# Softcapped attention feeding a mixture of causal attention experts: the exponentials of a pair of heads in one instruction, and a new order of score fills

## The chip, the cores and the metric

The kernel runs on one core of a Trainium2 chip. The metric is the time of the device for one execution, in microseconds (us); lower is better. The engines are named as in the profile: PE multiplies matrices (TensorE) and writes its results to PSUM, DVE (VectorE) and ACT (ScalarE) work elementwise, POOL (GpSimd) converts inputs and masks, and SP issues most loads and stores. Each engine works through its own queue in order; semaphores hold an instruction back until what it needs is there.

## The reference

Stage A is attention with a soft cap, for 8 batches and 12 heads of 448 tokens and 64 dimensions, cap 30:

```python
scores = scale * np.matmul(q, k.transpose(0, 1, 3, 2))
scores = cap * np.tanh(scores / cap)
attn = softmax(scores)            # exp, divided by its sum
x = matmul(attn, v)               # heads put side by side: (8, 448, 768)
```

Stage B treats each batch of x with four experts of one 64-wide head each: causal attention over projections of x, each token taking its two best experts, weighted by a softmax over their two gate values. The result is the sum of the weighted experts after an output projection, (8, 448, 768).

## The kernel before

**Pairs.** Stage A takes two heads at a time, 48 pairs, six to a batch. SP loads q, k and v of two pairs at once, some pairs ahead; POOL casts them to 16 bits (`a_cast`, L378, and `a_castv`, L399; pairs 0 and 1 partly on DVE); PE transposes queries and keys (`a_tr`, L410) and DVE moves the transposes to SBUF.

**Scores.** Scores lie with keys on the partitions and 448 queries along the row. Each head has three blocks of 128 keys; the remaining 64 keys of both heads make one shared "tail" block. So a pair has seven blocks of 448 columns. They are filled by PE in four parts (`fill`, L444): for a two-block part, one matmul per head, and each uses only the 64 partition rows on which its head's dimensions lie, one the lower and one the upper half; the tail is one matmul over all rows. A part occupies one of only two score buffers (`ps_score`, L280), two PSUM banks each. ACT reads a part with tanh (`tanh`, L462), which frees the buffer, and writes 16-bit values to SBUF; ACT then takes exp over several blocks at once (`expo`, L472). `HALF` (L441) gives the blocks of each part: 2, 2, 2, and the tail 1 last. Before the change a pair has two exponentials: over the four blocks of parts 0 and 1, and over the three of parts 2 and 3.

**ACT's order.** It is written out in the list `prog` (L894): T is a tanh, E an exp, X an exp of stage B, S marks where a new pair begins. For a common pair p:

```
T(p,0) T(p,1) [X part 0] E(p-1,1) [X part 1] T(p,2) T(p,3) E(p,0)
```

The X parts are there for two pairs of each batch (`EXPB`, L891). The first pair begins with nothing to finish; the last pair issues all four tanh, then the remaining three exponentials.

**After the exp.** PE multiplies the probabilities with the values (`a_pv_mm`, L481): for each of four query windows seven matmuls, six of a head's block and one of the tail with a value tile that holds both heads. A last value column of ones gives the sum; DVE takes its reciprocal and scales (`a_pv_out`, L516). PE transposes the result into x.

**Stage B.** For a finished batch PE computes projections for queries and keys of two experts at a time (r = 0, 1), values and gates. The causal scores of two experts e are filled into two score buffers of at most 1024 columns (`b_fill`, L675), laid out by `COL`: part 0 holds the tails and the three blocks of expert 0, part 1 the three blocks of expert 1. The experts of a pair lie on the two row halves of PE. ACT takes the exp (`b_exp`, L697), POOL zeroes what lies above the diagonal with `affine_select`, and products, transposes and the output projection follow, the last with a store by SP.

**The order on PE** comes from a planner that runs while the kernel is built (`Plan`, L18). It keeps an estimate of when each engine gets how far. For each score fill (`do_fill`, L920) it notes when the buffer comes free and when ACT will need it, and `pump` (L86) first issues other work through `step` (L65): of the units that could start soonest, the one with the earliest due time, as long as it ends before `latest`. `slot` (L943) and `batch` (L980) put units of stage A and B into the list with costs, dependencies and due times; loads and casts are issued in `slot` too. After the last pair's fills, `last_batch` (L1026) takes all that is left and orders it with a search over a list scheduler (`Graph`).

Of the kernel before, what the change touches and what calls it, by code (L numbers as in the profile page):

```python
# [11 lines left out]
f16 = mybir.dt.float16  # L12
# [5 lines left out]
class Plan:  # L18
# [46 lines left out]
    def step(self, until, latest):  # L65


        at = {}
        for u in self.work:
            r = self.ready(u)  # L70
            if r is not None:
                at[u["key"]] = max(r, self.pe)
        if not at:
            return False
        first = min(at.values())
        u = min(
            (u for u in self.work if at.get(u["key"], 1.0e9) <= first + 0.3),
            key=lambda u: u["due"],
        )
        if first > until or first + u["pe"] > latest:  # L80
            return False
        self.work.remove(u)
        self.emit(u)
        return True
# [156 lines left out]
def kernel(  # L241
# [199 lines left out]
    HALF = (2, 2, 2, 1)  # L441
    score = {}

    def fill(p, i):  # L444
        qt, kt = qkt[p]
        sc = ps_score.tile([128, 2, 512], f32, name=f"s{i}_{p}", tag="score")
        if i == KC:
            del qkt[p]
            nc.tensor.matmul(sc[:, 0, 0:S], kt[:, 0:128], qt, start=True, stop=True)  # L449
        else:  # L450
            for g in range(2):
                r = slice(64 * g, 64 * (g + 1))
                nc.tensor.matmul(  # L453
                    sc[:, g, 0:S], kt[r, 128 * (i + 1) : 128 * (i + 2)], qt[r, :],
                    start=True, stop=True,
                )
        score[(p, i)] = sc
# [4 lines left out]
    def tanh(p, i):  # L462
        g = i // 2
        n = HALF[i]
        if i % 2 == 0:
            y[(p, g)] = actp.tile([128, 4 - g, S], f16, name=f"y{g}_{p}", tag=f"y{g}", bufs=2)
        nc.scalar.activation(  # L467
            y[(p, g)][:, 2 * (i % 2) : 2 * (i % 2) + n, :], score.pop((p, i))[:, 0:n, 0:S],
            AF.Tanh, scale=isc / capf,
        )  # L470

    def expo(p, g):  # L472
        pt = actp.tile([128, 4 - g, S], f16, name=f"p{g}_{p}", tag=f"p{g}")
        nc.scalar.activation(pt, y.pop((p, g)), AF.Exp, scale=capf)  # L474
        pr[(p, g)] = pt
# [5 lines left out]
    def a_pv_mm(p, i, n, parts):  # L481

        if n == 0 and 0 in parts:
            pvs[p, i] = bank([128, 2, 2, Dh + 1], f32, f"pv{i}_{p}")
        pv = pvs[p, i]
        w = WIN[2 * i + n]
        for h in parts:
            pt = pr[(p, h)]
            for c in (2 * h, 2 * h + 1):
                if c == KC:  # L490
                    nc.tensor.matmul(  # L491
                        pv[:, n, :, :], pt[:, 2, w : w + 128], vtz[p % 12],
                        start=False, stop=True, skip_group_check=True,
                    )
                    continue
                for g in range(2):
                    nc.tensor.matmul(  # L497
                        pv[:, n, g, :], pt[:, 2 * (c % 2) + g, w : w + 128],
                        v16[p % 12][:, g, c, :],
                        start=(n == 0 and c == 0 and g == 0), stop=False, skip_group_check=True,  # L500
                    )
# [14 lines left out]
    def a_pv_out(p, i):  # L516
        a_pv_rc(p, i)
        a_pv_xk(p, i)
        if i == 1:
            del pr[(p, 0)], pr[(p, 1)]  # L520
# [152 lines left out]
    COL = {(0, 0): 64, (0, 1): 512, (0, 2): 832, (1, 1): 1024, (1, 2): 1344, (1, 0): 1536}  # L673

    def b_fill(b, r, g):  # L675
# [12 lines left out]

        if g == 0:
            for e in range(2):  # L690
                block(e, 0, KM, TL, 64 * e)
        for (e, c), o in COL.items():
            if e == g:
                block(e, o - 1024 * g, 128 * c, 128, 0)
        s["sc", r, g] = sc

    def b_exp(b, r, g):  # L697
# [3 lines left out]
        n = 1024 - 64 * g  # L701
        o0 = 64 + 1024 * g
# [3 lines left out]
        blocks = [(o, 0, 128, 128) for (e, _), o in COL.items() if e == g]  # L706
# [203 lines left out]
    def dur(o):  # L910
# [4 lines left out]
        return 0.09 + 0.373 * (4 - o[2]) if o[0] == "E" else 0.055 + 0.373 * HALF[o[2]]  # L915
# [4 lines left out]
    def do_fill():  # L920
# [3 lines left out]
        cost = 0.55 if o[0] == "X" else 0.5 if o[2] < KC else 0.19  # L924
# [3 lines left out]
        plan.pump(rel, at - cost - 0.4)  # L928
# [14 lines left out]
    def slot(p):  # L943
# [26 lines left out]
        if p == NP - 2:  # L970
            for r, w in EARLY:
                for j in range(4):
# [3 lines left out]
                        (*g, j), 0.19, 0.0, d, nom["E", p, 1] + j, qk_mm, r, w, j,  # L976
# [3 lines left out]
    def batch(b):  # L980
# [45 lines left out]
    def last_batch():  # L1026
# [49 lines left out]
        for u in (p - 1, p):  # L1076
            for i in range(2):
# [31 lines left out]
        for e in range(E):  # L1109
            if ("pvB", c, e) in left:  # L1110
                g = ("pvB", c, e)
                r = e // 2
                op((*g, 0), {"PE": 0.31}, [("X", c, r, e % 2)], b_pv_mm, c, e, group=g, opens=BOTH)
# [340 lines left out]
```

The softmax here doesn't subtract the row's maximum and nothing guards it: scores larger than these inputs give would overflow.

## Time and profile before

| quantity | value |
| --- | --- |
| median of 3 runs (lowest, highest) | 332.28 us (332.13, 333.07) |
| the profiled execution: own time | 332.43 us |
| the profiled execution: span, first to last instruction | 330.7 us |
| mean granted PE clock, share of full | 0.984 |

In rows of the page, the line is followed by the engine, the operation, what it writes and reads with shapes, the count, busy time in us and the mean duration in ns; then idle time of the engine ahead of it and what ended it. Durations include the start and the tail of an instruction, which overlap with its neighbours' on ACT and PE. A timeline row gives start and duration in us; neighbouring instructions of one group are merged into one row with a count. A row of windows gives the stretch, its length, busy time and count for each engine, the granted PE clock, and the share and rate of the DMA engines.

### The profile page before, as it was taken

The numbers are of one execution on the slowest core, as the hardware profiler recorded it, in microseconds if no ns is written. First come the engines' busy times: TensorE is split into PE (matmuls) and PEld (weight loads), VectorE is DVE, ScalarE is ACT, GpSimd is POOL, SyncE is SP. The second block draws the span as 40 slices with busy tenths as digits, with TensorE's granted clock in tenths as the row PEclk, the third lists the DMA queues.
The fourth block names the chain that finished last, engine by engine and source line by source line (L and its number), as shares of the span: only waits on it lengthen the run. The fifth ranks groups of instructions, "written<-read, shape, count | busy, mean of one in ns | idle before, by whom it ended". The sixth has DMA issues, their size and how long they took to land.

```text
span 330.7 us, 8813 instructions
## 1 busy us (share of the span) xinstructions
PE 279.7 (85%) x3335; PEld 177.4 (54%) x3335; DVE 212.2 (64%) x745; ACT 312.0 (94%) x353; POOL 156.0 (47%) x476
## 2 busy tenths in 40 slices
PE   5486589977889988998899889998798898898992
PEld 2254365555456564556655566556555565555861
DVE  4255445576557786668956688568855686646682
ACT  2989999999999999999999999999999999999592
POOL 3489999456707299765805285173912020022000
PEclk9999979999999999999999999999999999999997
DMA  7899999950363999477074903577003101120017
GB/s 165 214 247 246 216 222 233 211 116 3 87 177 88 285 264 258 145 195 179 3 217 158 287 13 108 156 216 192 3 7 138 24 3 50 50 71 3 2 74 261
DMA packets 65146, 46.19 MB, mean 140 GB/s; under 512 B 25872, under 2 KB 61584, under 8 KB 65104
## 3 DMA queue, kind: packets, MB, share of 16 engines
q1 hardware_dynamic: 54032, 43.58, 51.1%
q0 software_dynamic: 10512, 1.58, 6.7%
q8 instruction: 26, 0.43, 0.5%
q10 hardware_dynamic: 560, 0.48, 0.5%
q14 instruction: 16, 0.13, 0.1%
HBM read 36.19 MB, written 11.01 MB: 143 GB/s over the span
## 4 chain that ended last, share of the span: by engine, by line
ACT 81%; PE 7%; DMA 5%; POOL 3%; issue 1%; SPq 1%; DVEq 0%; ACTq 0%; POOLq 0%; DVE 0%
ACT y L467 38%; ACT p L474 35%; ACT pBs L703 8%; DMA ktf<-in_k_dram 3%; DMA kf<-in_k_dram 2%; PE wops L785 2%; POOL pBs L711 1%; PE vps L567 1%; PE kps L648 1%; PE qps L648 1%; POOL q L393 1%; PE pv L497 1%; POOL k L390 0%; POOL ktzs L389 0%; PE pvB L730 0%
## 5 line engine op out<-in xcount | busy, mean ns | idle before, releaser
L467 ACT ACTIVATE y<-s 128x896 f16<-128x896 f32 x192 | 152.7, 883 | 2.2 <-PE s L449 1.1
L474 ACT ACTIVATE p<-y 128x1792 f16<-128x1792 f16 x96 | 150.0, 1566 | 0.0
L711 POOL TENSOR_SCALAR_AFFINE_SELECT pBs<-pBs 128x128 f16<-128x128 f16 (+1 forms) x112 | 27.8, 278 | 123.6 <-ACT pBs L703 122.7
L453 PE MATMUL s<-qt,kt 64*128 64x448 f16 x288 | 52.5, 370 | 18.8 <-ACT y L467 14.5
L497 PE MATMUL pv<-v16s,p 128*128 128x65 f16 x1152 | 62.4, 196 | 5.9 <-ACT p L474 5.1
L497 PEld LDWEIGHTS <-p 128*128 128x128 f16 x1152 | 52.5, 99 | 24.7 <-issue 10.1
L453 PEld LDWEIGHTS <-kt 64*128 64x128 f16 x288 | 18.1, 94 | 47.8 <-issue 38.1
L511 DVE TENSOR_TENSOR xk<-pv,rc 128x256 f16<-128x256 f32 x96 | 40.6, 424 | 3.2
L491 PE MATMUL pv<-vtzs,p 128*128 128x130 f16 x192 | 42.0, 222 | 0.0
L507 DVE RECIPROCAL rc<-pv 128x4 f32<-128x4 f32 x96 | 17.1, 180 | 37.9 <-PE pv L491 37.0
L372 DVE COPY ob<-wops 128x384 f32<-128x384 f32 (+1 forms) x55 | 30.5, 554 | 9.1 <-PE wops L785 8.4
L785 PE MATMUL wops<-wo,oT 128*128 128x384 f16 x128 | 30.2, 326 | 0.0
L567 PE MATMUL vps<-wvg,xT 128*128 128x260 f16 (+1 forms) x192 | 29.8, 275 | 0.0
L703 ACT ACTIVATE pBs<-sB 128x1024 f16<-128x1024 f32 (+1 forms) x28 | 27.8, 992 | 0.7
L393 POOL CAST q<-qf 112x512 f16<-112x512 f32 x46 | 27.9, 607 | 0.0
L390 POOL CAST k<-kf 128x384 f16<-128x384 f32 x48 | 24.1, 502 | 6.8 <-DMA kf<-in_k_dram 3.9
L389 POOL CAST ktzs<-ktf 64x64 f16<-64x64 f32 x92 | 21.3, 232 | 9.1 <-DMA ktf<-in_k_dram 3.9
L684 PE MATMUL sB<-qe,ke 64*128 64x192 f16 (+2 forms) x112 | 18.3, 274 | 8.3 <-ACT y L467 4.7
L401 POOL CAST v16s<-vf 128x384 f16<-128x384 f32 x48 | 24.5, 510 | 1.2 <-DMA vf<-in_v_dram 1.0
L648 PE MATMUL qps<-xT,wq 128*128 128x448 f16 x96 | 24.9, 354 | 0.0
L648 PE MATMUL kps<-xT,wk 128*128 128x448 f16 x96 | 24.8, 353 | 0.0
L431 DVE COPY qt<-tps 128x384 f16<-128x384 f16 x48 | 16.8, 351 | 12.3 <-PE tps L421 12.3
(120 smaller groups left out, 456.7 us busy)
## 6 DMA issues: line engine op xcount, KB each, us to landing
qf<-in_q_dram SPq DMA_DIRECT2D x23, 448.0 KB, 5.6
out_dram<-ob SPq DMA_DIRECT2D x24, 384.0 KB, 2.9
kf<-in_k_dram SPq DMA_DIRECT2D x23, 384.0 KB, 6.4
vf<-in_v_dram SPq DMA_DIRECT2D x23, 384.0 KB, 5.8
ktf<-in_k_dram SPq DMA_DIRECT2D x46, 32.0 KB, 5.5
vtf<-in_v_dram SPq DMA_DIRECT2D x46, 32.0 KB, 5.1
out_dram<-ob SPq DMA_DIRECT2D x7, 192.0 KB, 2.9
qf<-in_q_dram ACTq DMA_DIRECT2D x2, 224.0 KB, 4.0
```

The costliest lines, as they stand in the source:

```text
L393: eng.tensor_copy(q16, qf.rearrange("p h (c d) -> p c h d", c=QC))
L453: nc.tensor.matmul(sc[:, g, 0:S], kt[r, 128 * (i + 1) : 128 * (i + 2)], qt[r, :], start=True, stop=True,)
L467: nc.scalar.activation(y[(p, g)][:, 2 * (i % 2) : 2 * (i % 2) + n, :], score.pop((p, i))[:, 0:n, 0:S], AF.Tanh, scale=isc / capf,)
L474: nc.scalar.activation(pt, y.pop((p, g)), AF.Exp, scale=capf)
L491: nc.tensor.matmul(pv[:, n, :, :], pt[:, 2, w : w + 128], vtz[p % 12], start=False, stop=True, skip_group_check=True,)
L497: nc.tensor.matmul(pv[:, n, g, :], pt[:, 2 * (c % 2) + g, w : w + 128], v16[p % 12][:, g, c, :], start=(n == 0 and c == 0 and g == 0), sto ...
L511: nc.vector.tensor_tensor(xt[p][:, 2 * i : 2 * i + 2, :, :], pv[:, :, :, 0:Dh], rc.broadcast_to((128, 2, 2, Dh)), ALU.mult,)
L567: nc.tensor.matmul(ps, xT[b][:, j, w : w + 128], wvg[:, j, 0 : ps.shape[1]], start=(j == 0 and first), stop=(j == NDC - 1), skip_group_che ...
L648: nc.tensor.matmul(ps, w2[r][:, j, :], xT[b][:, j, :], start=(j == 0), stop=(j == NDC - 1), skip_group_check=(b == B - 1),)
L703: nc.scalar.activation(pb[:, o0 : o0 + n], st[b].pop(("sc", r, g))[:, 0:n], AF.Exp, scale=isc)
L711: nc.gpsimd.affine_select(out=blk, in_=blk, compare_op=ALU.is_ge, fill=0.0, base=0, pattern=[[1, n]], channel_multiplier=-1,)
L785: nc.tensor.matmul(ps, st[b]["oT", r][:, w : w + 128], wo2[r][:, f * (D // 2) : (f + 1) * (D // 2)], start=(r == 0), stop=(r == 1),)
```

## The change

- `HALF` becomes 1, 2, 2, 2: the tail block is the first part of a pair instead of the last.
- All seven blocks of a pair share one tanh tile and, for pairs 0 to 46, one exp instruction of 3136 columns. The last pair keeps two exponentials, over three and four blocks (`PARTS`). The SBUF tiles have as many bytes as the two kinds had before together.
- The exp of pair p-1 is issued after the tail tanh of pair p. A common pair is now `T(p,0) E(p-1) [X part 0] T(p,1) [X part 1] T(p,2) T(p,3)`; for p = 1 the exp comes first.
- The product with the values starts with the tail block and becomes ready with the single exp.
- In stage B the first part holds tails and first key blocks of both experts (960 columns), the second the other two blocks of both (1024). The fills of the two experts alternate, so that neighbouring matmuls use different row halves. Products of any expert wait for the second part.
- The planner skips units that would not end before `latest` rather than stopping at the first of them; its cost of a fill and its margin ahead of a fill change, as do some due times.

The core of the diff (in `last_batch` and in `pump`'s callers only names of dependencies change further):

```diff
...
         at = {}
         for u in self.work:
             r = self.ready(u)
-            if r is not None:
+            if r is not None and max(r, self.pe) + u["pe"] <= latest:
                 at[u["key"]] = max(r, self.pe)
         if not at:
             return False
...
             (u for u in self.work if at.get(u["key"], 1.0e9) <= first + 0.3),
             key=lambda u: u["due"],
         )
-        if first > until or first + u["pe"] > latest:
+        if first > until:
             return False
         self.work.remove(u)
         self.emit(u)
...
-    HALF = (2, 2, 2, 1)
+    HALF = (1, 2, 2, 2)
+    PARTS = {p: [(0, 7)] if p < NP - 1 else [(0, 3), (3, 7)] for p in range(NP)}
+    def part(p, i):
+        o = sum(HALF[0:i])
+        g = max(g for g, (lo, _) in enumerate(PARTS[p]) if lo <= o)
+        return g, o - PARTS[p][g][0]
     score = {}
     def fill(p, i):
         qt, kt = qkt[p]
         sc = ps_score.tile([128, 2, 512], f32, name=f"s{i}_{p}", tag="score")
-        if i == KC:
-            del qkt[p]
+        if i == 0:
             nc.tensor.matmul(sc[:, 0, 0:S], kt[:, 0:128], qt, start=True, stop=True)
         else:
             for g in range(2):
                 r = slice(64 * g, 64 * (g + 1))
                 nc.tensor.matmul(
-                    sc[:, g, 0:S], kt[r, 128 * (i + 1) : 128 * (i + 2)], qt[r, :],
+                    sc[:, g, 0:S], kt[r, 128 * i : 128 * (i + 1)], qt[r, :],
                     start=True, stop=True,
                 )
+        if i == KC:
+            del qkt[p]
         score[(p, i)] = sc
     y = {}
     pr = {}
     def tanh(p, i):
-        g = i // 2
+        g, o = part(p, i)
         n = HALF[i]
-        if i % 2 == 0:
-            y[(p, g)] = actp.tile([128, 4 - g, S], f16, name=f"y{g}_{p}", tag=f"y{g}", bufs=2)
+        if o == 0:
+            y[(p, g)] = actp.tile([128, 7, S], f16, name=f"y{g}_{p}", tag="y", bufs=2)
         nc.scalar.activation(
-            y[(p, g)][:, 2 * (i % 2) : 2 * (i % 2) + n, :], score.pop((p, i))[:, 0:n, 0:S],
-            AF.Tanh, scale=isc / capf,
+            y[(p, g)][:, o : o + n, :], score.pop((p, i))[:, 0:n, 0:S], AF.Tanh,
+            scale=isc / capf,
         )
     def expo(p, g):
-        pt = actp.tile([128, 4 - g, S], f16, name=f"p{g}_{p}", tag=f"p{g}")
-        nc.scalar.activation(pt, y.pop((p, g)), AF.Exp, scale=capf)
+        n = PARTS[p][g][1] - PARTS[p][g][0]
+        pt = actp.tile([128, 7, S], f16, name=f"p{g}_{p}", tag="p")
+        nc.scalar.activation(pt[:, 0:n, :], y.pop((p, g))[:, 0:n, :], AF.Exp, scale=capf)
         pr[(p, g)] = pt
     xt = {}
...
             pvs[p, i] = bank([128, 2, 2, Dh + 1], f32, f"pv{i}_{p}")
         pv = pvs[p, i]
         w = WIN[2 * i + n]
-        for h in parts:
-            pt = pr[(p, h)]
-            for c in (2 * h, 2 * h + 1):
-                if c == KC:
-                    nc.tensor.matmul(
-                        pv[:, n, :, :], pt[:, 2, w : w + 128], vtz[p % 12],
-                        start=False, stop=True, skip_group_check=True,
-                    )
-                    continue
-                for g in range(2):
-                    nc.tensor.matmul(
-                        pv[:, n, g, :], pt[:, 2 * (c % 2) + g, w : w + 128],
-                        v16[p % 12][:, g, c, :],
-                        start=(n == 0 and c == 0 and g == 0), stop=False, skip_group_check=True,
-                    )
+        for j in (0, 1) if 0 in parts else ():
+            blk(p, pv, n, w, j)
+        for j in (2, 3) if 1 in parts else ():
+            blk(p, pv, n, w, j)
+    def blk(p, pv, n, w, j):
+        h, o = part(p, j)
+        pt = pr[(p, h)]
+        if j == 0:
+            nc.tensor.matmul(
+                pv[:, n, :, :], pt[:, o, w : w + 128], vtz[p % 12], start=(n == 0),
+                stop=False, skip_group_check=True,
+            )
+            return
+        for g in range(2):
+            nc.tensor.matmul(
+                pv[:, n, g, :], pt[:, o + g, w : w + 128], v16[p % 12][:, g, j - 1, :],
+                start=False, stop=(j == KC), skip_group_check=True,
+            )
     def a_pv_rc(p, i):
         if p not in xt:
...
-    COL = {(0, 0): 64, (0, 1): 512, (0, 2): 832, (1, 1): 1024, (1, 2): 1344, (1, 0): 1536}
+    COL = {(0, 0): 64, (1, 0): 512, (0, 1): 960, (0, 2): 1280, (1, 1): 1472, (1, 2): 1792}
+    XCOL = (0, 960, 1984)
     def b_fill(b, r, g):
         s = st[b]
...
                 stop=True,
             )
+        for c in (1, 2) if g else (0,):
+            for e in range(2):
+                block(e, COL[e, c] - XCOL[g], 128 * c, 128, 0)
         if g == 0:
             for e in range(2):
                 block(e, 0, KM, TL, 64 * e)
-        for (e, c), o in COL.items():
-            if e == g:
-                block(e, o - 1024 * g, 128 * c, 128, 0)
         s["sc", r, g] = sc
     def b_exp(b, r, g):
         assert b < 2 or ("pvB", b - 2, E - 1) in plan.done
         pb = pB[2 * (b % 2) + r]
-        n = 1024 - 64 * g
-        o0 = 64 + 1024 * g
+        n = XCOL[g + 1] - XCOL[g]
+        o0 = 64 + XCOL[g]
         nc.scalar.activation(
             pb[:, o0 : o0 + n], st[b].pop(("sc", r, g))[:, 0:n], AF.Exp, scale=isc
         )
-        blocks = [(o, 0, 128, 128) for (e, _), o in COL.items() if e == g]
+        blocks = [(o, 0, 128, 128) for (_, c), o in COL.items() if (c > 0) == g]
         if g == 0:
             blocks += [(0, 0, 64, 64), (0, 64, 128, 64)]
         for o, r0, r1, n in blocks:
...
     prog = []
     for p in range(NP):
         t = [("T", p, i) for i in range(4)]
-        e1 = [("E", p - 1, 1)] if p else []
+        e = [("E", p - 1, 0)] if p else []
         x = [("X", *EXPB[p], g) for g in range(2)] if p in EXPB else []
         prog.append(("S", p))
-        if p < NP - 1:
-            prog += t[0:2] + x[0:1] + e1 + x[1:2] + t[2:4] + [("E", p, 0)]
-        else:
-            prog += t + e1 + [("S", NP), ("E", p, 0), ("E", p, 1)]
+        prog += e + t if p == 1 else t[0:1] + e + x[0:1] + t[1:2] + x[1:2] + t[2:4]
+    prog += [("S", NP), ("E", NP - 1, 0), ("E", NP - 1, 1)]
     reads = [o for o in prog if o[0] in "TX"]
     where = [i for i, o in enumerate(prog) if o[0] in "TX"]
     ends = {}
...
             return 0.0
         if o[0] == "X":
             return 0.9
-        return 0.09 + 0.373 * (4 - o[2]) if o[0] == "E" else 0.055 + 0.373 * HALF[o[2]]
+        if o[0] == "E":
+            return 0.09 + 0.373 * (PARTS[o[1]][o[2]][1] - PARTS[o[1]][o[2]][0])
+        return 0.055 + 0.373 * HALF[o[2]]
     def fill_dep(o):
         return (("tr", o[1]),) if o[0] == "T" else (("q", o[1], o[2]), ("k", o[1], o[2]))
...
         nonlocal nfill
         o = reads[nfill]
         rel = ends[nfill - 2] if nfill >= 2 else 0.0
-        cost = 0.55 if o[0] == "X" else 0.5 if o[2] < KC else 0.19
+        cost = 0.42 if o[0] == "X" or o[2] else 0.19
         for d in fill_dep(o):
             plan.force(d)
         at = plan.act + sum(dur(x) for x in prog[pos : where[nfill]])
-        plan.pump(rel, at - cost - 0.4)
+        plan.pump(rel, at - cost - 0.3)
         plan.pe = max(plan.pe, rel, *(plan.done[d] for d in fill_dep(o))) + cost
         fill(*o[1:]) if o[0] == "T" else b_fill(*o[1:])
         plan.done[("f", nfill)] = plan.pe + plan.LAT
...
         for i in (1, 2) if p == 0 else ahead(p, TR, DEEP + 4, 4):
             plan.add(("tr", i), 0.43, 0.95, [("cast", i)], nom["T", i, 0] - 3.0, a_tr, i)
         if 1 <= p < NP:
-            es = [("E", p - 1, 0), ("E", p - 1, 1)]
-            due = nom["S", p + 1] if p < NP - 1 else nom["E", p - 1, 1]
+            es = [("E", p - 1, 0)]
+            due = nom["S", p + 1] + 2.0 if p < NP - 1 else nom["E", p, 0]
             plan.parts(("pv", p - 1, 0), 2, 0.47, 0.55, es, due, a_pv, p - 1, 0)
             d = [("pv", p - 1, 0)]
             plan.parts(("pv", p - 1, 1), 2, 0.47, 0.55, d, due, a_pv, p - 1, 1)
...
         plan.add(("g", b), 0.0, 0.8, [("g1", b), ("G", b)], t1 + 3.0, b_gate2, b, aux=None)
         for e in range(E):
             due = t1 + 6.0 + 3.0 * e
-            d = [("X", b, e // 2, e % 2), ("g", b)] + [("pvB", b, e - 1)] * (e % 2)
+            d = [("X", b, e // 2, 1), ("g", b)] + [("pvB", b, e - 1)] * (e % 2)
             plan.add(("pvB", b, e), 0.31, 0.7, d, due, b_pv, b, e)
             if e % 2:
                 plan.add(("oT", b, e // 2), 0.22, 0.35, [("pvB", b, e)], due, b_ot, b, e // 2)
...
                     for n in range(2):
                         op(
                             (*g, h, n), {"PE": 0.12},
-                            [("E", u, h)] + [(*g, h - (n == 0), 1 - n)] * (h + n > 0),
+                            [("E", u, h * (u == p))] + [(*g, h - (n == 0), 1 - n)] * (h + n > 0),
                             a_pv_mm, u, i, n, (h,), group=g, opens=BOTH if h + n == 0 else None,
                         )
                 op((*g, "rc"), {"DVE": 0.18}, [(*g, 1, 1)], a_pv_rc, u, i, group=g)
...
```

More of the change, by code (lines that the diff above doesn't have):

```diff
@@ L519, in a_pv_out @@
         if i == 1:
-            del pr[(p, 0)], pr[(p, 1)]
+            for g in range(len(PARTS[p])):
+                del pr[(p, g)]
     def a_pv(p, i, n):
@@ L975, in slot @@
                     plan.add(
-                        (*g, j), 0.19, 0.0, d, nom["E", p, 1] + j, qk_mm, r, w, j,
+                        (*g, j), 0.19, 0.0, d, nom["E", NP - 1, 0] + j, qk_mm, r, w, j,
                         aux="open" if j == 0 else None, group=g,
@@ L1112, in last_batch @@
                 r = e // 2
-                op((*g, 0), {"PE": 0.31}, [("X", c, r, e % 2)], b_pv_mm, c, e, group=g, opens=BOTH)
+                op((*g, 0), {"PE": 0.31}, [("X", c, r, 1)], b_pv_mm, c, e, group=g, opens=BOTH)
                 op((*g, 1), {"DVE": 0.18}, [(*g, 0)], b_pv_rc, c, e, group=g)
```

## The prediction

> **What bounds the kernel now.** I read the page first: busy shares, then the chain that ended last, then the costliest groups.
>
> ```profile
> PE 279.7 (85%) x3335; PEld 177.4 (54%) x3335; DVE 212.2 (64%) x745; ACT 312.0 (94%) x353; POOL 156.0 (47%) x476
> ...
> ACT 81%; PE 7%; DMA 5%; POOL 3%; issue 1%; SPq 1%; DVEq 0%; ACTq 0%; POOLq 0%; DVE 0%
> ...
> L467 ACT ACTIVATE y<-s 128x896 f16<-128x896 f32 x192 | 152.7, 883 | 2.2 <-PE s L449 1.1
> L474 ACT ACTIVATE p<-y 128x1792 f16<-128x1792 f16 x96 | 150.0, 1566 | 0.0
> ```
>
> ACT is busy 94% of the span and carries 81% of the last chain; tanh (L467) and exp (L474) are its work and hardly ever start after an idle stretch. So time is won by fewer or shorter ACT instructions, or by closing waits which the busy figures hide. For both I need starts, not durations: neighbours overlap, so the cost of one is the distance to the next start. The timeline of ACT:
>
> ```profile
> 154.66 1.72 ACT L474 ACTIVATE p<-y 128x1792 f16<-128x1792 f16 x1
> 156.25 1.74 ACT L467 ACTIVATE y<-s 128x896 f16<-128x896 f32 x2
> 157.85 1.36 ACT L474 ACTIVATE p<-y 128x1344 f16<-128x1344 f16 x1
> 159.06 1.39 ACT L467 ACTIVATE y<-s 128x896 f16<-128x896 f32 x2
> ```
>
> The exp of four blocks occupies 156.25 - 154.66 = 1.59 us, that of three 159.06 - 157.85 = 1.21. A block of 448 columns costs the difference, 0.373 (rounded up, 0.38); three of them are 1.12, so an exp has a fixed cost of 0.09. Two tanh of 896 take 1.60, 0.80 each.
>
> A hidden wait stands where stage B's first exp follows two tanh (ACT, then PE):
>
> ```profile
> 148.62 0.97 ACT L467 ACTIVATE y<-s 128x896 f16<-128x896 f32 x1
> ...
> 149.64 0.73 PE L684 MATMUL sB<-qe,ke 64*64 64x64 f16 x5 [0.64 <-DVE mske L613]
> ...
> 150.46 1.02 ACT L703 ACTIVATE pBs<-sB 128x1024 f16<-128x1024 f32 x1
> 151.38 1.31 ACT L474 ACTIVATE p<-y 128x1344 f16<-128x1344 f16 x1
> ```
>
> The first tanh ends at 149.59 and frees a score buffer; 0.05 later PE starts the five fills of the part, ends them 0.73 later at 150.37, and 0.09 after that the exp starts. Two tanh should take 1.60, but 150.46 - 148.62 is 1.84: 0.24 us late. The same two starts at all fourteen such places give 0.19 to 0.35 late, 3.87 us in all. The page shows 0.7 idle there, because the preceding tanh's tail covers the rest.
>
> The end belongs to PE (windows; columns: span, PE busy, clock, DMA share, GB/s):
>
> ```profile
> 304.00:309.10 5.10, 5.09 (x98) 1.00 0.00 0
> 309.10:324.90 15.80, 15.36 (x195) 1.00 0.27 89
> ```
>
> From the last score fill at 304.01 on, PE is practically never idle.
>
> **The change, part by part.** *One exp instead of two.* For pairs 0 to 46 one instruction goes: 47 x 0.09 = 4.3. ACT stands still for 1.12 us around 17 us, waiting for a fill behind transposes of freshly cast inputs; what the first two pairs save is lost in that wait. 45 x 0.093 (0.09 before rounding is between 0.092 and 0.093) = **-4.2**. At that wait the new order has one block less behind it (0.37), and the next wait, 0.39 at 23 us, falls away because its tanh stands later: nought together. Nothing is added on ACT: the 3136-column exp should take 7 x 0.373 + 0.09 = 2.71. It reads what the last tanh of its pair wrote; the tail tanh issued between them (0.42) is longer than that tanh's trailing 0.17, so no wait. Pair 0's exp has no such cover, but lies ahead of the 17 us wait.
>
> *The stage B exp.* Its first part now stands behind the long exp, 2.71 us of cover, so the wait of fourteen parts goes: **-3.9**. Its second part (1024 columns) now stands one tanh behind the first: the buffer comes free at that exp's end (0.96), plus 0.05, plus the fill, plus 0.09; it is due after 0.85 + 0.80 = 1.65. The fill of three blocks in one row half took 0.58 (the row at 150.88). With 320 and 192 columns in both halves side by side I take 0.40: 0.96 + 0.05 + 0.40 + 0.09 = 1.50, in time by 0.15. Were the halves served one after the other it would be about 0.62, 0.07 late, 1.0 for fourteen. The two score matmuls of 64 rows start 6 ns apart and 0.37 covers both (row below), so I take side by side and allow **+0.2**. The four mask operations behind the second part are one more than before (0.25 us of POOL); only stage B's next products wait for them, not ACT.
>
> *Four tanh in a row.* This is what the change pays with. Before, an exp stood between every two tanh, and each score fill had over 1.6 us from its buffer's release until it was needed. Now the fill of the fourth tanh and that of the next pair's tail have only one tanh of 0.80. The nearest row for the loop is the one above, with the score fill in place of stage B's:
>
> ```profile
> 157.24 0.37 PE L453 MATMUL s<-qt,kt 64*128 64x448 f16 x2 [0.18 <-ACT y L467]
> ```
>
> 0.97 + 0.05 + 0.37 + 0.09 = 1.48 against 1.60: in time by 0.12 if PE is free at the release. So PE's queue decides. I counted, in the built order of instructions, what stands between the fourth block's fill and the next tail's fill: nothing in 6 of 47 pairs, up to 0.5 us of work in 22, 0.5 to 0.67 in 19 (14 PV matmuls at 0.49, two projections at 0.38, three value matmuls at 0.34). After 1.02 + 0.30 for the fill, 0.67 ends at 1.99; fill 0.35 and 0.09 make 2.43 against 2.39: 0.04 late at worst. 19 x 0.04 = **+0.8**. Between tail fill and the next fourth fill PE has 4.72 of ACT time less 0.78 of fills, and holds at most 4.15 in pairs with stage B parts, where ACT adds 1.8 more: fits. Bounds: below, nothing; above, 0.1 at each of 94 fills (a DVE or ACT result one operation late in front of the fill), 9.4.
>
> A rule that speaks against the change: the clock. Windows (PE, PEld, DVE, ACT, POOL busy, then PE's clock):
>
> ```profile
> 37.70:41.10 3.40, 1.62 (x20) 1.11 (x20) 1.03 (x5) 3.40 (x6) 3.23 (x7) 0.91 1.52 221
> 40.50:43.90 3.40, 3.17 (x35) 2.34 (x31) 1.36 (x5) 3.40 (x5) 3.34 (x8) 0.50 1.51 232
> ```
>
> After a stretch with PE busy 1.62 of 3.40 the clock is halved for 3.4 us. The Trainium skill, "TensorE: Matmul & The Clock Gate", section "HAM oscillation — how this bites in real kernels", puts the condition as no idle gap above about 3.4 us. Here no gap near 40 us exceeded 0.75, and the clock fell: a thin stretch suffices, and the row decides. The new order gathers PE's idle time under the 2.71 us exp, worst in pairs 2 to 7, which have no stage B work. By the page this costs nothing; by the row, fills lengthen from 0.36 to about 0.55, which turns 0.12 of slack into 0.06 late, and for the tail fill 0.03: 6 x 0.09 = **+0.5**, which I take.
>
> *The end.* Behind the last score fill stand 291 matmuls, 288 before. That fill is released by the pair's second tanh; behind it ACT had 0.80 + 0.42 + 1.21 + 1.59 + 1.21 = 5.23 left and now has 1.60 + 1.21 + 1.59 = 4.40. As PE sets the end, 0.83 of ACT's gain does not arrive; the planner's order of the last batch may give some back: **+0.7**, bounds 0 and 1.3.
>
> *Other edits at nothing.* The new test in the planner's step only chooses what PE does between fills; the moved tail block changes PV's order, not its count; SP's loads and POOL's casts are issued at the same slots.
>
> Sum: -4.2 - 3.9 + 0.2 + 0.8 + 0.5 + 0.7 = -5.9. The profiled execution has a span of 330.7 and its own time is 332.43, 1.7 around it, which the change does not touch; 324.8 + 1.7 = 326.5, and as the median shown is 0.15 below the profiled one, **326.4**.
>
> **Rivals.** *PE late at the tight fills (slower).* Place: the fourth tanh and the next tail tanh of each pair. For: PE is at 85%, and one late DVE result in front of a fill passes on to ACT undiminished. Against: the counted work fits, and before, PE itself waited for ACT at score fills for over 12 us, so it usually arrives early. ACT loses what exceeds 0.12. Gains without these terms are 4.2 + 3.9 - 0.2 - 0.7 = 7.2; over 94 fills this breaks even when PE is 0.20 late on average. At 0.24 late, 11.3 - 7.2 = 4.1 slower: 336.4.
>
> *POOL holds the first third.* For: POOL is busy 3.2 to 3.3 of 3.4 in the windows above, and inputs pass through it. Against: after 23 us no ACT wait there. If it paces up to 100 us, 14 pairs x 0.09 and four waits of 0.27 are lost, 2.4: 328.8.
>
> *The clock falls in stage B pairs too.* If 25 more pairs run their tight window at half clock, with the work between fills doubled as well, about 0.13 each: +3.2, 329.6. Against: there PE is busy over 80%.
>
> *Stage B's halves don't run side by side:* +1.0 - 0.2, 327.2; the long exp still removes the first wait.
>
> *All terms at their lower end:* nothing late, tail arriving whole: -8.1, 324.2.
>
> **How the numbers follow.** The forecast and its neighbours (halves one after the other; lower end) 0.68; POOL 0.07; clock 0.12; PE late but still a gain, 330 to 331.2, 0.02; within 0.3%, 0.02; slower 0.09. About 0.3% (1.0 us) is what a measurement here can tell from no change. So faster 0.89, same 0.02, slower 0.09. The range reaches from the lower end, 324.2, to beyond the clock rival, 330.0; the likeliest case's own range is 324.2 to 328.2.
>
> **What would show it.** Right: 47 exp of 3136 columns with 2.71 us to the next start; 0.80 between tanh also for the fourth and the next tail; the first stage B part starting at the end of the exp's 2.71, the second 1.65 behind it; 26 to 27 us from the second tanh of pair 47 to the end. Wrong: a group of tanh with several us of idle released by PE score fills, and PE rows in front of them that wait for DVE or POOL; half clock in many slices; ACT waiting for score fills in the first 100 us behind casts; a tail longer than 27 us.

## The result

The changed kernel takes 327.14 us (median of 5 runs, 326.63 to 327.23) against 332.28 (331.46 to 333.07): ratio 0.9841, 95% interval 0.9822 to 0.9861. That is 5.1 us or 1.6% faster. Forecast were 326.4 and 5.9. The profiled execution has its own time of 327.23 and a span of 325.5.

The page after, busy shares, chain, and the two groups of ACT:

```profile
PE 276.0 (85%) x3335; PEld 178.2 (55%) x3335; DVE 214.4 (66%) x745; ACT 306.9 (94%) x306; POOL 155.8 (48%) x476
...
ACT 75%; PE 12%; issue 6%; DMA 3%; DVE 1%; SPq 1%; POOL 0%
...
L477 ACT ACTIVATE y<-s 128x448 f16<-128x448 f32 x192 | 152.9, 960 | 2.2 <-PE s L461 1.7
L485 ACT ACTIVATE p<-y 128x3136 f16<-128x3136 f16 (+2 forms) x49 | 141.5, 2895 | 0.0
```

Exp has 47 fewer instructions and 8.5 us less busy time; tanh is where it was. But ACT's share of the last chain fell from 81 to 75% and PE's rose from 7 to 12: PE has become a second bound.

ACT's timeline over a pair with stage B parts:

```profile
145.08 2.94 ACT L485 ACTIVATE p<-y 128x3136 f16<-128x3136 f16 x1
147.79 1.09 ACT L721 ACTIVATE pBs<-sB 128x960 f16<-128x960 f32 x1
148.64 1.05 ACT L477 ACTIVATE y<-s 128x896 f16<-128x896 f32 x1
149.43 1.17 ACT L721 ACTIVATE pBs<-sB 128x1024 f16<-128x1024 f32 x1
150.34 1.07 ACT L477 ACTIVATE y<-s 128x896 f16<-128x896 f32 x1
```

The exp of seven blocks occupies 147.79 - 145.08 = 2.71 us, as worked out. The first part starts right behind it, the second 1.64 later, as worked out too, and its fill is as short as assumed (PE, same stretch):

```profile
148.93 0.40 PE L702 MATMUL sB<-qe,ke 64*128 64x320 f16 x4 [0.79 <-ACT pBs L721]
```

The old 0.24 us gap is gone, and so are its thirteen fellows. In their place stand short waits at the tight score fills. In the start times between 24 and 300 us, tail tanh start late at eleven places, by 0.04 to 0.16 and 1.0 in all. Two-block tanh are late by 0.36 and 0.09 at 76 and 77 us, second parts by 0.20 in all at three places; with many delays below 0.04 it comes to about 2.2 us, against 1.5 that I had allowed. One late tail, PE and then ACT:

```profile
130.31 0.36 PE L461 MATMUL s<-qt,kt 64*128 64x448 f16 x2 [0.16 <-ACT y L477]
130.61 0.50 PE L803 MATMUL wops<-wo,oT 128*128 128x384 f16 x2
130.95 0.50 PE L583 MATMUL vps<-wvg,xT 128*128 128x260 f16 x3
131.28 0.35 PE L457 MATMUL s<-qt,kt 128*128 128x448 f16 x1
```
```profile
129.10 1.17 ACT L477 ACTIVATE y<-s 128x896 f16<-128x896 f32 x1
...
130.72 1.17 ACT L477 ACTIVATE y<-s 128x896 f16<-128x896 f32 x1
131.67 0.65 ACT L477 ACTIVATE y<-s 128x448 f16<-128x448 f32 x1
```

The tail starts 0.95 behind the tanh before it instead of 0.80. PE had idled 0.16 ahead of the fill at 130.31 and then did exactly the 0.67 us of work that the order puts in front of the tail's fill. The release had come late: the tanh at 129.10, whose end freed the buffer for the fill at 130.31, lasts 1.17, where 0.92 to 0.97 had gone into the sum. Worked out from these rows, either a tanh of 0.92 or an empty PE queue would have had the tail in time; it takes both to make it late. What these durations mean is the main thing that the runs taught.

In the profiled executions the last score fill starts at 298.76 instead of 304.01, 5.25 earlier, and the tail behind it takes 26.73 us instead of 26.70. So the gain up to that fill arrives whole at the end. ACT itself gained more: behind that fill it has 0.83 less left than before, and its last exponential ends at 303.10 instead of 309.21, but PE still needs as long from the fill on.

### The profile page after: what moved, and what is told of

The parts are those of the page before. It is cut to its first block, busy times and chain, and to the rows that moved or that the text cites. A ratio compares the mean times of both kernels' runs of the same rounds, so it can differ in the third digit from the quotient of the medians.

```text
span 325.5 us, 8764 instructions
## 1 busy us (share of the span) xinstructions
PE 276.0 (85%) x3335; PEld 178.2 (55%) x3335; DVE 214.4 (66%) x745; ACT 306.9 (94%) x306; POOL 155.8 (48%) x476
## 3 DMA queue, kind: packets, MB, share of 16 engines
q0 software_dynamic: 10512, 1.58, 6.9%
## 4 chain that ended last, share of the span: by engine, by line
ACT 75%; PE 12%; issue 6%; DMA 3%; DVE 1%; SPq 1%; POOL 0%
ACT y L477 37%; ACT p L485 29%; ACT pBs L721 8%; DMA ktf<-in_k_dram 3%; PE wops L803 2%; PE s L461 1%; PE pv L513 1%; PE kps L664 1%; PE vps L583 1%; PE tps L414 1%; PE xtp L548 1%; PE pvB L748 1%; PE pv L507 1%; SPq L316 1%; PE qps L664 1%
## 5 line engine op out<-in xcount | busy, mean ns | idle before, releaser
L477 ACT ACTIVATE y<-s 128x448 f16<-128x448 f32 x192 | 152.9, 960 | 2.2 <-PE s L461 1.7
L485 ACT ACTIVATE p<-y 128x3136 f16<-128x3136 f16 (+2 forms) x49 | 141.5, 2895 | 0.0
L513 PE MATMUL pv<-v16s,p 128*128 128x65 f16 x1152 | 60.6, 196 | 0.0
L513 PEld LDWEIGHTS <-p 128*128 128x128 f16 x1152 | 52.3, 99 | 4.2 <-ACT p L485 0.3
L507 PE MATMUL pv<-vtzs,p 128*128 128x130 f16 x192 | 43.3, 226 | 11.5 <-ACT p L485 8.6
L461 PEld LDWEIGHTS <-kt 64*128 64x128 f16 x288 | 19.3, 93 | 31.6 <-issue 21.5
L507 PEld LDWEIGHTS <-p 128*128 128x128 f16 x192 | 18.8, 98 | 29.6 <-ACT p L485 17.4
L721 ACT ACTIVATE pBs<-sB 128x960 f16<-128x960 f32 (+1 forms) x28 | 32.0, 1141 | 0.0
```

The lines of the kernel that those rows point to most:

```text
L461: nc.tensor.matmul(sc[:, g, 0:S], kt[r, 128 * i : 128 * (i + 1)], qt[r, :], start=True, stop=True,)
L477: nc.scalar.activation(y[(p, g)][:, o : o + n, :], score.pop((p, i))[:, 0:n, 0:S], AF.Tanh, scale=isc / capf,)
L485: nc.scalar.activation(pt[:, 0:n, :], y.pop((p, g))[:, 0:n, :], AF.Exp, scale=capf)
L507: nc.tensor.matmul(pv[:, n, :, :], pt[:, o, w : w + 128], vtz[p % 12], start=(n == 0), stop=False, skip_group_check=True,)
L513: nc.tensor.matmul(pv[:, n, g, :], pt[:, o + g, w : w + 128], v16[p % 12][:, g, j - 1, :], start=False, stop=(j == KC), skip_group_check=True,
L721: nc.scalar.activation(pb[:, o0 : o0 + n], st[b].pop(("sc", r, g))[:, 0:n], AF.Exp, scale=isc)
```

## Experiments

The theory to test had three parts: one exp saves 4.2 to 4.3 us, covering stage B's first part saves 3.9, and PE arriving late at tight fills (or at half clock) takes some back. The growing durations of tanh suggested a rival for the last two, called "lag" below: each ACT instruction's end slips a little behind the start of its successor, so starts alone misstate its cost, and a "wait" can be this lag being made good. The first four kernels ran beside 11 runs of the kernel before, median 331.98.

**Stage B's layout alone**, in the kernel before.

```diff
-    COL = {(0, 0): 64, (0, 1): 512, (0, 2): 832, (1, 1): 1024, (1, 2): 1344, (1, 0): 1536}
+    COL = {(0, 0): 64, (1, 0): 512, (0, 1): 960, (0, 2): 1280, (1, 1): 1472, (1, 2): 1792}
...
-        cost = 0.55 if o[0] == "X" else 0.5 if o[2] < KC else 0.19
+        cost = 0.42 if o[0] == "X" else 0.5 if o[2] < KC else 0.19
...
```

> The kernel before with only stage B's new layout and interleaved fills (and their planner cost); two exponentials and the old order stay. Theory 'starts' (start-to-start distances are the whole cost of ACT): the fill ahead of stage B's first part shrinks from 0.73 to about 0.45 us, so of the fourteen waits of 0.19 to 0.35 only about 0.3 us in all stays; 3.5 us faster than before, 328.8. Theory 'lag' (each tanh's end slips about 10 ns further behind the start of its successor until ACT has to wait; about 1.7 of the 3.9 us were this lag being made good): only about 2.2 faster, 330.1, with waits of 0.1 or so remaining. Rival 'not side by side': fills stay at 0.7, no change.

Measured: 330.33, ratio 0.9948 (0.9928 to 0.9969), 1.7 faster. The fill did shrink (PE, then ACT):

```profile
149.06 0.51 PE L685 MATMUL sB<-qe,ke 64*128 64x448 f16 x4 [0.64 <-DVE mske L613]
```
```profile
148.00 1.81 ACT L467 ACTIVATE y<-s 128x896 f16<-128x896 f32 x2
149.68 1.00 ACT L704 ACTIVATE pBs<-sB 128x960 f16<-128x960 f32 x1
```

0.51 instead of 0.73, yet the exp still starts 0.08 late (1.68 for two tanh of 0.80). The fourteen waits sum to 2.2 us, 0.04 to 0.21 each but for one of 0.79 at 74.56; "starts" left 0.3. The long one stands right behind a stretch at half clock (70.4 to 73.8), in which PE was busy 3.32 of 3.41 us. The other thirteen waits shrank by 2.25 us, 0.17 each, for a fill shortened by 0.22: by less than that, as "lag" has it, though the whole gain is 0.5 below the 2.2 that "lag" forecast. The halves do run side by side.

**Stage B's parts behind the exps**, in the kernel before.

```diff
-            prog += t[0:2] + x[0:1] + e1 + x[1:2] + t[2:4] + [("E", p, 0)]
+            prog += t[0:2] + e1 + x[0:1] + t[2:4] + [("E", p, 0)] + x[1:2]
...
```

> The kernel before with old layout and two exponentials, only ACT's order changed: stage B's two parts stand behind an exp each (first behind the exp of three blocks, second behind that of four), so both fills have over 1.2 us of cover. 'Starts': the fourteen waits vanish, 3.9 faster, 328.4. 'Lag': the starts gain 3.9, but the lag then grows to over 1 us, or is made good where a score fill waits for a tanh's end; about 2.2 faster, 330.1, and the durations of tanh grow well beyond the 1.14 us of before.

Measured: 336.95, ratio 1.0162 (1.0122 to 1.0203), slower, which neither theory said. The run tells nothing between them. The planner orders PE by ACT's order, so this edit changed both at once: 369 matmuls are left behind the last score fill, against 288 before. The order on ACT alone stays untested in the kernel before.

**Two exponentials again**, in the changed kernel at the same place.

```diff
-    PARTS = {p: [(0, 7)] if p < NP - 1 else [(0, 3), (3, 7)] for p in range(NP)}
+    PARTS = {p: [(0, 3), (3, 7)] for p in range(NP)}
...
-        e = [("E", p - 1, 0)] if p else []
+        e = [("E", p - 1, g) for g in range(2)] if p else []
...
```

> The changed kernel with the exp of every pair cut in two again (three and four blocks, back to back at the same place). All theories: 46 more instructions at 0.093, 4.3 slower than the changed kernel, 331.4; with the lag, a little less (3.8), as an exp makes good some 10 ns of it.

Measured: 329.26, ratio 0.9918 (0.9893 to 0.9942), some 2.2 slower than the changed kernel, half of what all theories said. In the profiles the last score fill starts at 302.34, 3.58 later than in the changed kernel, so on ACT most of the price shows. But the tail behind it takes 24.42 us instead of 26.73: with 3.6 us more under ACT, PE got through more of its work ahead of that fill and has 238 matmuls left, not 291. So PE pays back half of ACT's price by the medians, and 2.3 of 3.6 by the profiles; the profiled execution was 0.7 faster than this run's median. With two exponentials the new order is worth little on ACT: the last one ends at 306.70, in the run with the layout alone at 307.13.

**The old layout** in the changed kernel.

```diff
-    COL = {(0, 0): 64, (1, 0): 512, (0, 1): 960, (0, 2): 1280, (1, 1): 1472, (1, 2): 1792}
+    COL = {(0, 0): 64, (0, 1): 512, (0, 2): 832, (1, 1): 1024, (1, 2): 1344, (1, 0): 1536}
...
-        cost = 0.42 if o[0] == "X" or o[2] else 0.19
+        cost = 0.55 if o[0] == "X" else 0.42 if o[2] else 0.19
...
```

> The changed kernel with stage B's old layout and serial fills. The second part (three blocks of one expert in one row half, fill about 0.58 to 0.62) now stands one tanh behind the first. 'Starts': 0.07 late at fourteen places, 1.0 slower than the changed kernel, 328.1. 'Lag': the ends are 0.1 to 0.25 later than fresh ones, so 0.2 late each, partly in place of waits at score fills; 1.5 to 2.5 slower, 328.6 to 329.6.

Measured: 328.16, ratio 0.9889 (0.9867 to 0.9911), 1.0 slower than the changed kernel's 327.14 by the medians and 1.6 by the ratios. The two intervals don't overlap, and the fastest execution here (327.60) is slower than the slowest there (327.23), so it is slower, but by an amount that does not tell the two theories apart. The second part's waits sum to 1.65 us over fourteen places, more than the 1.0 of "starts"; in exchange only 0.17 of tail waits are left past the start-up. Its last fill starts at 298.06, 0.7 earlier than in the changed kernel, and its tail, with 302 matmuls, takes 27.81, 1.1 longer. So behind the long exp the new layout shows its worth in the tail and not on ACT. All late starts between 24 and 300 us sum to 4.1 us before, 2.5 with the layout alone, 2.3 here and 2.1 to 2.2 in the changed kernel: the two parts of the change close the same wait, and either does most of it alone.

**ACT by itself.** This kernel leaves out all but a chain of ACT instructions (80 tanh of 896 columns, 40 exps of 1792, 16 times the new sequence) and stores zeros.

```python
for i in range(80):
    tanh(i, 1 + 2 * (i // 4 % 3), 2, i)
for i in range(40):
    expo(i, 4)
for i in range(16):
    tanh(i, 0, 1, i)
    expo(i + 3, 7)
    for o in (1, 3, 5):
        tanh(i, o, 2, o)
```

> Only ACT instructions and a store of zeros, nothing of the reference: 80 tanh of 896 columns from PSUM, 40 exps of 1792 columns, then 16 times the changed kernel's sequence (tanh 448, exp 3136, three tanh 896), without PE and without a wait that is not long fulfilled. 'Lag': starts keep 0.797 apart while each end slips 10 to 13 ns further (by 80 tanh up to 1.0 us), or, if the lag is bounded, the starts spread to about 0.81 once the bound is reached; the exps make some 3 to 10 ns good each. 'Starts': the lag stays at 0.12 to 0.18 throughout, and its growth in the kernel comes from PE or DVE using PSUM at the same time.

Its tanh, with duration in ns as minimum, median and maximum:

```profile
L55 ACT ACTIVATE y<-s x80: 912/1399/1926, 7.2 to 75.1; 128x896 f16<-128x896 f32 x80
```

After three separate ones, starts stay 0.797 apart throughout while the duration grows from 0.91 to 1.93 us, by 13 ns each, with no other engine at work. Of the 40 exps from SBUF that follow, the first 25 make good 12 ns each, the rest 2. In the mixed sequence the lag settles near 0.4: there the exp, which reads what the fourth tanh wrote, waits for that end past the tail tanh of 0.42 between them, and the starts spread (tail 0.445 instead of 0.423, exp 2.723 instead of 2.707). So the ends do slip without any other engine, as "lag" has it, and they are real ends, for the exp waits for one. The kernels show both sizes too: in the changed kernel's profile a tanh adds 13 ns and a long exp takes 11 off, in the kernel before and with two exponentials a tanh adds 10 and an exp takes 2 off. What decides between the two no run tells.

**A larger planner margin** in the changed kernel, so that less work stands before a tight fill.

```diff
-        plan.pump(rel, at - cost - 0.3)
+        plan.pump(rel, at - cost - 0.35)
```

> The changed kernel with a larger planner margin ahead of each score fill (0.35 instead of 0.3), so that less work is put in front of a tight fill. 'PE late': the waits at the tail tanh (1.15 us over twelve places) fall to 0.3 or less. 'Lag': they stay at 0.9 or more, since the release itself is late. Either way 262 matmuls stand behind the last score fill instead of 291; if the tail goes by that count (24.4 us at 238, 26.7 at 291), it takes 25.5, 1.2 less. Together 325.2 with 'PE late', 326.0 with 'lag'.

Measured: 326.90, ratio 0.9841 (0.9808 to 0.9875), beside 12 runs of the kernel before as the next two, median 332.74. That is the same as the changed kernel; both theories had said faster. Past the start-up the tail waits fell from 1.0 to 0.40 us over six places, near what "PE late" forecast and far from "lag". But those at stage B's second part rose from 0.20 to 0.72, so that the two together went only from 1.2 to 1.1. So less work in front of a tight fill does relieve it, and most of the wait comes up again elsewhere. The tail took 26.25 with 262 matmuls, 0.5 less, not 1.2.

**Both parts behind the exp** in the changed kernel.

```diff
-        prog += e + t if p == 1 else t[0:1] + e + x[0:1] + t[1:2] + x[1:2] + t[2:4]
+        prog += e + t if p == 1 else t[0:1] + e + x + t[1:4]
```

> The changed kernel with stage B's second part directly behind the first (both behind the long exp), so its fill has the exp's cover and no tight place of its own; the first two-block tanh after it is due 0.90 later with a fill of 0.37. The waits at and behind the second part (0.57 us in all) go; 0.3 to 0.6 faster than the changed kernel, 326.6 to 326.8, the tail unchanged (291 matmuls behind the last fill).

Measured: 327.97, ratio 0.9862 (0.984 to 0.9884), no gain where 0.3 to 0.6 was forecast. The second part's waits vanished, and tail waits past the start-up rose from 1.0 to 1.3 us: again the sum stayed, the place moved.

**The exp one tanh later** in the changed kernel.

```diff
-        prog += e + t if p == 1 else t[0:1] + e + x[0:1] + t[1:2] + x[1:2] + t[2:4]
+        prog += e + t if p == 1 else t[0:2] + e + x[0:1] + t[2:3] + x[1:2] + t[3:4]
...
```

> The changed kernel with each long exp one place later, behind the tail tanh and the first two-block tanh. Then the next pair's second fill is released by the fourth tanh's end and due only a tail tanh of 0.42 later: 0.92 to 0.97 + 0.05 + 0.37 + 0.09 against 0.80 + 0.42, 0.21 to 0.26 late in each of 46 pairs, 9.7 to 12 in all; less the waits that the changed kernel has at tight fills (about 2). 7 to 10 slower than the changed kernel, 334 to 337; 332 matmuls behind the last fill would add 3.

Measured: 334.61, ratio 1.0067 (1.0043 to 1.0091), 7.5 slower than the changed kernel, within the forecast. Every one of 46 pairs waits at the tanh behind the tail, nearly all of them 0.15 to 0.17 and the longest 0.34, 7.6 us in all. That is less than the 9.7 to 12 forecast, and a longer tail makes up for it, so the total agrees in part by luck. One pair:

```profile
165.72 0.92 ACT L477 ACTIVATE y<-s 128x896 f16<-128x896 f32 x1
...
166.51 0.56 ACT L477 ACTIVATE y<-s 128x448 f16<-128x448 f32 x1
...
167.09 0.92 ACT L477 ACTIVATE y<-s 128x896 f16<-128x896 f32 x1
```

167.09 - 166.51 is 0.58 for a tail of 0.42. These tanh have the fresh duration of 0.92: a wait in each pair leaves no lag to build up. The loop is then 0.92 + 0.05 + 0.36 + 0.05, the last term from the fill's end to the tanh being 0.05 here and not 0.09. The tail took 30.4 us with 332 matmuls, 3.7 more than in the changed kernel, and the last fill starts 3.6 later. The exp's place right behind the tail is worth these 7.5 us.

**Stage B's second pair of experts one pair of heads earlier** in the changed kernel, chosen because it leaves 238 matmuls behind the last fill; below it the changed kernel once more. Both beside 11 runs of the kernel before, median 332.39.

```diff
-    EXPB = {HP * (b + 1) + 3 + 2 * r - (b == B - 2) * r: (b, r) for b in range(B - 1) for r in range(2)}
+    EXPB = {HP * (b + 1) + 3 + r: (b, r) for b in range(B - 1) for r in range(2)}
```

> The changed kernel with the second expert pair's stage B parts one pair of heads after the first's, not two (the last batch already has that), which lets stage B's later work go earlier. In the built order 238 matmuls stand behind the last score fill instead of 291. 'The tail goes by the work left to PE': 24.4 us after the last fill (as measured at 238 with two exponentials) instead of 26.7, the last fill within 0.5 of the changed kernel's 298.8; 2.3 faster, 324.8, the fastest so far. Rival 'the tail is set by the latency behind the last exponential': no change, 327.1.

> The changed kernel once more, unaltered, beside the run above on the same chip: 327.1, ratio to the kernel before 0.984.

Measured: 327.19, ratio 0.9829 (0.98 to 0.9857), and 327.02, ratio 0.9834 (0.9808 to 0.986): no difference. The tail shrank to 25.33, between the two theories (238 matmuls took 24.42 with two exponentials), but the last fill came 1.3 later, at 300.08. Three waits of 0.46 to 0.51 explain it; ahead of each PE ran at half clock. Windows of the first (columns as before):

```profile
148.20:151.60 3.40, 1.58 (x36) 1.20 (x33) 2.89 (x12) 3.40 (x4) 3.07 (x11) 1.00 0.00 0
151.60:155.00 3.40, 3.40 (x37) 2.36 (x37) 2.08 (x9) 3.40 (x3) 3.05 (x10) 0.50 0.02 5
```

After a stretch with PE busy 1.58 of 3.40 us the clock is halved for one stretch, PE falls behind, and the fill at 156.95 is late. The repeated kernel shows the same at a place where the first execution of this program had no fall (PE, then ACT):

```profile
151.15 0.30 PE L507 MATMUL pv<-vtzs,p 128*128 128x130 f16 x1
151.25 0.54 PE L513 MATMUL pv<-v16s,p 128*128 128x65 f16 x6
151.59 0.56 PE L457 MATMUL s<-qt,kt 128*128 128x448 f16 x1
```
```profile
150.98 1.09 ACT L477 ACTIVATE y<-s 128x896 f16<-128x896 f32 x1
152.19 0.54 ACT L477 ACTIVATE y<-s 128x448 f16<-128x448 f32 x1
```

The clock fell at 150.9; the tail's fill takes 0.56 instead of 0.35 and its tanh starts 1.21 behind the one before instead of 0.80. In the first profile of the changed kernel stretches at half clock began at 29, 39 and 70 us. The waits behind the first two are below 0.03 each, but the third cost 0.45. The same stretches show it, in the first profile and then in the repeated one:

```profile
66.74:70.15 3.41, 1.76 (x29) 1.29 (x27) 3.14 (x13) 3.41 (x4) 2.63 (x8) 1.00 0.74 175
70.15:73.57 3.42, 3.42 (x41) 2.50 (x39) 1.66 (x8) 3.42 (x4) 0.00 (x0) 0.50 0.00 0
```
```profile
66.74:70.15 3.41, 1.77 (x31) 1.29 (x29) 3.17 (x14) 3.41 (x4) 2.50 (x8) 1.00 0.67 168
70.15:73.57 3.42, 2.54 (x50) 1.92 (x46) 2.73 (x12) 3.42 (x4) 0.00 (x0) 1.00 0.02 5
```

In the first, PE then idles in front of an output transpose that waits for DVE, with a score fill behind it, and the tanh after stage B's second part starts 1.27 behind it; in the repeated one it starts 0.91 behind it, as it should (PE and ACT of the first, then ACT of the repeated one):

```profile
75.64 0.34 PE L548 MATMUL otp<-ident,osc 128*128 128x128 f16 x3 [0.59 <-DVE osc L772]
```
```profile
75.11 1.23 ACT L721 ACTIVATE pBs<-sB 128x1024 f16<-128x1024 f32 x1
76.38 0.92 ACT L477 ACTIVATE y<-s 128x896 f16<-128x896 f32 x1
```
```profile
74.96 1.23 ACT L721 ACTIVATE pBs<-sB 128x1024 f16<-128x1024 f32 x1
75.87 1.13 ACT L477 ACTIVATE y<-s 128x896 f16<-128x896 f32 x1
```

The repeated one pays at other places: in or just behind its half-clock stretches four tanh are late by 0.18 to 0.42, 1.16 in all. Yet both have their last fill within 0.1 of each other. The repeated one leaves the start-up 0.28 earlier, and after its wait of 0.42 later fills are late by 0.19 less, since a wait also makes good lag.

## Why the prediction was right, and where it was off

Time and sign were right: 327.14 lies in the likeliest case's own range. The gain was 0.7 smaller than forecast. By the steps of the sum, to the last score fill and its tail:

- *One exp instead of two, -4.2.* The starts bear it out: 46 exps of 2.707 against 1.586 + 1.213, 4.2 us. Two exponentials measured 3.58 at the last fill, 0.6 less. Lag made good by the added exps explains at most a sixth of that, as they gave back only 2 ns each there; that this profiled execution was 0.7 faster than its median could, which is not shown.
- *The stage B exp, -3.9, with +0.2 for its second part.* The wait went, as said, and the first part needs no new layout for it (the old-layout run). But its length was taken for its worth. In the kernel before, tanh durations grow along an unbroken run of ACT and fall back at these waits:

```profile
25.84 0.92 ACT L467 ACTIVATE y<-s 128x896 f16<-128x896 f32 x1
...
59.52 1.13 ACT L467 ACTIVATE y<-s 128x896 f16<-128x896 f32 x1
...
64.45 0.92 ACT L467 ACTIVATE y<-s 128x896 f16<-128x896 f32 x1
```

  Summed over the run the lag grew by 1.7 us there, nearly all of it made good inside the fourteen waits. So about 2.1 of the 3.87 was waiting that a shorter or covered fill can remove.
- *Four tanh in a row, +0.8.* With the clock's +0.5 and the second part's +0.2 this made 1.5, and 2.2 was measured: the term that was mis-sized. The mechanism was named as PE's work in front of a fill, and the margin run shows that to be a part. What the sum lacked is the late release: 0.97 + 0.05 + 0.37 + 0.09 took a duration near its beginning, and at 1.17 it exceeds the 0.80 + 0.80 at hand. How the 2.2 divides is not shown. It is about what the lag would grow to over the run (0.04 a pair, 1.9, and 28 stage B exps at 0.013, 0.4), and the runs that moved waits left their sum nearly as it was. But in the margin run the tail waits fell by more than half, which the release alone would not allow.
- *The clock, +0.5.* Right in size by luck. In the first profile two of the three half-clock stretches lay in the pairs forecast and cost next to nothing; the third lay in a pair with stage B parts and cost 0.45. In the repeated kernel it was 1.16 in all. The mean clock says nothing here (0.959 against 0.984 before), as five executions of the changed kernel had 0.959 to 0.988. And that a thin stretch suffices was too simple a reading: with PE busy 1.76 of 3.41 us the clock fell in one execution (without an idle gap above 1.05), with 1.77 in the same place it stayed in the other.
- *The end, +0.7.* 0.83 by the position of the fill, and the tail is 26.73 against 26.70: right, 0.13 small.

Sum by what was measured in starts: -4.2 - 3.9 + 2.2 + 0.8 = -5.1, against -5.2 in span. The start-up is nought to within about 0.1: ACT resumes 0.39 earlier, one block (0.37) behind. But the wait at 23 us did not fall away, as the prediction had it: 0.35 of it stayed, of 0.51 between starts before.

Of the rivals, POOL left no mark in the first third beyond the start-up. PE late on average by 0.2, the slower case, didn't come: PE waited for ACT's releases 33 times at two-block fills, 9.8 us in all. The clock rival happens at single places only. What I did not see is how near PE is to being the bound: the two-exp run shows that half to two thirds of ACT's gain from the single exp comes back in the tail as PE work not yet done. Against the kernel before this was hidden because both leave nearly the same count (288 and 291).

Left open: what inside ACT makes the ends slip. The exps of stage B, which read 32-bit values from PSUM, slip by 10 to 13 ns like tanh, while the exps that read 16-bit values from SBUF gain; that points to the source and not to the function, but no run varied memory or type alone. Nor is it known what lets the clock fall behind one thin stretch and not behind another.

## What to carry to other kernels

Read the cost of an instruction from starts, but take the release of a buffer from ends, and look at whether durations of one form grow along a busy stretch: a wait that resets them is partly a debt being paid, and removing it returns less than its length. Before giving a queue longer runs of instructions that share two buffers, add up the loop of end, signal, refill and signal against the distance between starts, at the duration late in such a run. When the bounding engine is made faster, count what the second engine has left behind the last handover, and compare kernels by where that handover stands and by what follows it. Read the place of a clock fall from more than one execution before giving it a price.

## What the runs showed of the hardware

- In a chain of ACT instructions alone, 78 tanh of 896 columns from PSUM started 0.797 us apart while each end slipped 13 ns further, to 1.93 us of duration; of the exps from SBUF behind them the first 25 gave back 12 ns each, the rest 2. In the kernel before a tanh slipped 10 ns and an exp gave back 2.
- PE's clock was halved for 3.4 us or more after stretches with PE busy 1.6 to 2.2 of 3.4 us; in the kernel before no idle gap exceeded 0.75 us in two such stretches. Stretches as thin also passed without it: 2.17 of 3.40 at 27.4 us there, and 1.77 of 3.41 in the repeated kernel. The same program had its half-clock stretches at different times in two executions.
- Two matmuls of 64 rows in the two row halves ran side by side: four fills of stage B's second part, 1024 columns, took 0.40 us; three in one half, 960 columns, 0.58.
